# The last pair of heads moves into TensorE's loop, and two weight matrices are loaded ahead of its values

## Chip, cores and metric

One core of a Trainium2 chip. The time is that of one execution on the device in microseconds, as the median of several; the kernel before takes 687.5 us (three runs, 687.22 to 687.5). Everything is computed in f32.

## The reference, cut to what matters

```python
def _A_ref(x, k_cache, v_cache, wq, wo):          # x: 1 x 1 x 512; caches: 1 x 32 x 8192 x 128
    q = (x @ wq).reshape(B, Sq, H, Dh).transpose(0, 2, 1, 3)
    scores = jnp.einsum("bhqd,bhkd->bhqk", q, k_cache) * (Dh ** -0.5)
    p = _softmax(scores, axis=-1)
    o = jnp.einsum("bhqk,bhkd->bhqd", p, v_cache)
    return o.transpose(0, 2, 1, 3).reshape(B, Sq, H * Dh) @ wo

def _B_ref(x, w_gate, w_up, w_down):              # 512 x 1376, 512 x 1376, 1376 x 512
    h = _sigmoid(x @ w_gate) * (x @ w_up)
    return h @ w_down

xn = _layernorm(x)
return x + _A_ref(xn, ...) * _silu(_B_ref(xn, ...))
```

It decodes one token: attention of 32 heads over a cache of 8192 positions, times the silu of a gated unit. The two caches hold 268 MB of the 294 MB that are read.

## The kernel before

**Stages.** The heads are worked on in 16 pairs (NP = 16). A pair's keys and a pair's values are 8.39 MB each, laid out as 128 partitions of 64 KB, and fill one of three slots in the on-chip memory. Keys of pair i go to `slots[i % 2]`, values always to `slots[2]`, but for the last pair's. For each pair VectorE (DVE) multiplies the keys by the query and reduces (`scores`, L281 and L282; `summed[i]` marks the end and so that the slot of these keys is free). TensorE (PE) and ScalarE (ACT) make the maximum and the powers. PE multiplies 32 blocks of values by the weights into the PSUM bank `po` (L255, two passes for f32: 64 matmuls in the trace) and signals `valued`; ACT copies `po` to `o1` (`parts`, L301), PE picks the two heads' sums out of it (L260), DVE divides (`heads_out`), and ACT issues two small transfers that put the result into four partitions each of `o_all` (`place`, L131 on ACT's queue). The function `pair` holds PE's part. It runs 15 times in a hardware loop on PE and once more written out behind the loop.

**Order of the loads.** All large loads are issued by SP, in program order, each behind the wait that says that its slot is free:

```python
wait(SP, summed[NP - 2])
SP.dma_start(slots[NP % 2], rows_of(v_cache, NP - 1)).then_inc(v_last, 16)
...
ld_g = load(SP, "wg", wg_t, w_gate..., (valued, NP - 1))
```

So the last values go to `slots[0]`, free since the scores of pair 14 are done, and follow the values of pair 14 in the stream. Behind them come gate's matrix (2752 KB), up's (2752 KB) and down's (2560 KB, and its last 128 rows, 256 KB, again as `wd_last`) into `slots[2]`, which wait for the values of pair 14 to be used. Then the output matrix wo (8192 KB) in six pieces that end at rows 14, 24, 28, 30, 31 and 32 of each partition (`W_ENDS`), into `slots[1]`, which wait for the scores of pair 15. The program counts `valued` and `summed` so that `(valued, NP - 1)` is the end of pair 14's values.

**The end.** Behind the last pair PE multiplies by gate and up (L356; 64 matmuls of 320 columns and 48 of 32), DVE and ACT make the hidden vector and transpose it (L360 to L367), PE multiplies it by down (L384), ACT copies the four partial rows, PE folds them (L377, 8 matmuls) and the gate factor is made. Then PE waits for `placed[15]`, that is for `o_all`, and multiplies by wo piece by piece (L402 for rows 0 to 27 with 512 columns, four partial rows; a copy by ACT and a fold; L406 for rows 28 to 31 with 128 columns), each as it lands. DVE multiplies by the gate factor and adds x (L416, L418), and SP stores 2 KB.

Of the kernel before, what the change touches and what calls it, by code (L numbers as in the profile page):

```python
# [9 lines left out]
AF = mybir.ActivationFunctionType  # L10
# [3 lines left out]
P = 128  # L14
# [4 lines left out]
def kernel(  # L19
# [12 lines left out]
    nc = tc.nc  # L32
    _, H, S, Dh = k_cache.shape
    D = x.shape[-1]
    F = w_gate.shape[1]
    KT = D // P
    HP = P // 2
    NB = S // HP
    NP = H // 2
    NG = 4  # L40
    GP = P // NG
    GC = D // NG
    QT = 512
    HT = QT // Dh
    NQ = H * Dh // QT
# [6 lines left out]
    FP = F // P  # L52
    FL = F - FP * P
    FW = FP * GP
    FH = FW + GP
    assert FH <= QT and FL % GP == 0 and 2 * KT * F + FP * D <= SLOT

    W_ENDS, W_FOLD = (14, 24, 28, 30, 31, 32), 28

    PE, DVE, ACT, SP, POOL = nc.tensor, nc.vector, nc.scalar, nc.sync, nc.gpsimd  # L60
# [15 lines left out]
    x_col, xc, sq, xn = (sb(n, KT) for n in ("x_col", "xc", "sq", "xn"))  # L76
# [4 lines left out]
    slots = [sb(f"slot{i}", SLOT) for i in range(3)]  # L81
    x_row, g_row = sb("x_row", GC), sb("g_row", GC)
# [6 lines left out]
    wd_last = q_all[:, :D]  # L89
    sg, hg, s_tmp = (q_all[:, a:a + n] for a, n in ((D, FH), (D + FH, FH), (D + 2 * FH, QT)))  # L90
    assert D + 2 * FH + QT <= NP * Dh and FH <= QT

    weights = sb("weights", NB // HT, 2 * HT)
# [3 lines left out]
    hid = o1[:, :(FP + 1) * GP].rearrange("p (c i) -> p c i", i=GP)  # L97

    o_all = sb("o_all", WR)

    big = [bank(f"big{i}", P, QT) for i in range(2)]
    acc, po = bank("acc", P, GC), bank("po", P, QT)
# [6 lines left out]
    def semaphore(name):  # L109
        sems.append(nc.alloc_semaphore(name))  # L110
        return sems[-1]
# [11 lines left out]
    pe, dve, act, pool = (Steps(n) for n in ("s_pe", "s_dve", "s_act", "s_pool"))  # L123
    loads = {}

    def load(eng, name, dst, src, *after):
        wait(eng, *after)
        if name not in loads:
            loads[name] = [semaphore(f"s_{name}"), 0]
        loads[name][1] += 16  # L130
        eng.dma_start(dst, src).then_inc(loads[name][0], 16)  # L131
        return loads[name][0], loads[name][1]

    def wait(eng, *steps):
        for s in steps:
            if s is not None:
                eng.wait_ge(*s)


    turned, spread_m, valued, picked = (semaphore(f"s_{n}") for n in ("turned", "spread", "valued", "picked"))  # L140
    maxed, reduced, powers, copied = (semaphore(f"s_{n}") for n in ("maxed", "reduced", "powers", "copied"))
    s_val = semaphore("s_val")
# [6 lines left out]
    def rows_of(src, i):  # L149
        rows = src.rearrange("b h s d -> (b h s) d")[2 * i * S:2 * (i + 1) * S, :]  # L150
        return rows.rearrange("(p j) d -> p (j d)", p=P)
# [6 lines left out]
    def load_values(i, *after):  # L158

        wait(SP, *after)  # L160
        SP.dma_start(slots[2], rows_of(v_cache, i)).then_inc(s_val, 16)
# [10 lines left out]
    c_id = pool(POOL.memset(ident, 0.0))  # L172
    wait(POOL, c_id)
    c_id = pool(POOL.affine_select(out=ident, in_=ident, compare_op=ALU.not_equal, fill=1.0, base=0,
                                   pattern=[[-1, P]], channel_multiplier=1))
# [4 lines left out]
    t = dve(DVE.reduce_sum(st[:, 0:1], x_col, axis=AX.X))  # L180
    wait(PE, t)
    t = pe(PE.matmul(pt[:, 0:1], ones, st[:, 0:1], start=True, stop=True))  # L182
# [3 lines left out]
    t = dve(DVE.tensor_scalar(xc, x_col, st[:, 1:2], None, op0=ALU.subtract))  # L186
# [53 lines left out]
    def taken(sem, n):  # L240
        PE.wait_ge(sem, n)
        PE.nop().then_inc(sem, -n)  # L242

    def pair(v, loaded):
        taken(maxed, 1)
        PE.matmul(pt[0:1, :], mx[:, 0:1], ident, start=True, stop=True).then_inc(turned, 1)  # L246
        taken(reduced, 1)
        PE.matmul(pm, ones[:1, :], mx[:1, 1:3], start=True, stop=True).then_inc(spread_m, 1)  # L248
        taken(powers, 2)
        PE.matmul(pn[:, Dh:], half, rs, start=True, stop=True)  # L250
        loaded()

        for j in range(0, NB, HT):
            g = j // HT % NG
            ins = PE.matmul(po[g * GP:g * GP + 2 * HT, :], weights[:, j // HT, :], v[:, j * Dh:(j + HT) * Dh],  # L255
                            start=(j < HT * NG), stop=(j >= NB - HT * NG))
        ins.then_inc(valued, 1)
        taken(copied, 1)
        for b in range(HT):
            ins = PE.matmul(pn[:, :Dh], pick[:, b:2 * HT:HT], o1[:, b * Dh:(b + 1) * Dh],  # L260
                            start=(b == 0), stop=(b == HT - 1))
        ins.then_inc(picked, 1)

    wait(PE, c_pick, c_id)
    with nc.Fori(0, NP - 1, engines=OrderedEngineSet([PE.engine]), head_slot={PE.engine: 0}):
        pair(slots[2], lambda: taken(s_val, 16))

    v_last = semaphore("s_v_last")
    pair(slots[NP % 2], lambda: PE.wait_ge(v_last, 16))


    summed, outs, placed = {}, {}, {}
# [54 lines left out]
    place(NP - 1)  # L327


    wait(SP, summed[NP - 2])  # L330
    SP.dma_start(slots[NP % 2], rows_of(v_cache, NP - 1)).then_inc(v_last, 16)
    t = slots[2]
    wg_t, wu_t = (t[:, n * KT * F:(n + 1) * KT * F].rearrange("p (k f) -> p k f", f=F) for n in range(2))
    wd_t = t[:, 2 * KT * F:2 * KT * F + FP * D].rearrange("p (c e) -> p c e", e=D)
    ld_g = load(SP, "wg", wg_t, w_gate.rearrange("(p k) f -> p k f", k=KT), (valued, NP - 1))
    ld_u = load(SP, "wu", wu_t, w_up.rearrange("(p k) f -> p k f", k=KT))
    load(SP, "wd", wd_t, w_down[:FP * P, :].rearrange("(p r) e -> p r e", r=FP))
    ld_d = load(SP, "wd", wd_last, w_down[F - P:, :])
    wo_t = slots[(NP - 1) % 2].rearrange("p (r e) -> p r e", e=D)
    ld_o = []  # L340
    for n, (r0, r1) in enumerate(zip((0,) + W_ENDS, W_ENDS)):
# [1 line left out]
                         summed[NP - 1] if n == 0 else None))  # L343


    g0 = (P - FL) // GP
    wait(DVE, copies[NQ - 1])
    c_zero = dve(DVE.memset(big[1][:g0 * GP, FW:FH], 0.0))
    wait(PE, c_zero)
    rows = []  # L350
    for dst, src, ld in ((big[0], wg_t, ld_g), (big[1], wu_t, ld_u)):
        wait(PE, ld)
        for c0, f0, w, g1 in ((0, 0, FW, 0), (FW, F - P, GP, g0)):
            for k in range(KT):
                for g in range(g1, NG):
                    ins = PE.matmul(dst[g * GP:g * GP + 1, c0:c0 + w], xn[:, k:k + 1],  # L356
                                    src[:, k, f0 + g * w:f0 + (g + 1) * w], start=(k == 0), stop=(k == KT - 1))
        rows.append(pe(ins))
    wait(ACT, rows[0])
    t = act(ACT.activation(sg, big[0][:, :FH], AF.Sigmoid))  # L360
    wait(DVE, t, rows[1])
    c_p4 = dve(DVE.memset(big[0], 0.0))
    t = dve(DVE.tensor_mul(hg, sg, big[1][:, :FH]))
    wait(DVE, t)
    for c in range(FP):
        dve(DVE.transpose(hid[:, c, :], hg[:, c:FW:FP]))
    t = dve(DVE.transpose(hid[:, FP, :], hg[:, FW:]))  # L367

    def to_fold(after):
        wait(ACT, after)  # L370
        return act(ACT.copy(s_tmp, big[0]))

    def fold(dst, copied, last):

        wait(PE, copied)
        for g in range(NG):
            ins = PE.matmul(dst[g * GP:g * GP + 1, :GC], ones[:, 0:1], s_tmp[:, g * GC:(g + 1) * GC],  # L377
                            start=last, stop=last)
        return ins

    wait(PE, t, ld_d)
    for c in range(FP + 1):
        g = c % NG * GP
        ins = PE.matmul(big[0][g:g + 1, :], hid[:, c, 0:1], wd_t[:, c, :] if c < FP else wd_last,  # L384
                        start=(c < NG), stop=(c + NG > FP))
    t = to_fold(pe(ins))
    wait(DVE, t)
    c_acc4 = dve(DVE.memset(big[0], 0.0))
    wait(ACT, pe(fold(big[1], t, True)))
    t = act(ACT.activation(g_row, big[1][:, :GC], AF.Sigmoid))  # L390
    wait(DVE, t)
    c_gate = dve(DVE.tensor_mul(g_row, g_row, big[1][:, :GC]))


    wait(PE, c_acc4, placed[NP - 2], placed[NP - 1])
    r0, parts = 0, None
    for ld, r1 in zip(ld_o, W_ENDS):
        wait(PE, ld)
        for r in range(r0, r1):
            if r < W_FOLD:  # L400
                g = r % NG * GP
                ins = PE.matmul(big[0][g:g + 1, :], o_all[:, r:r + 1], wo_t[:, r, :],  # L402
                                start=(r < NG), stop=(r + NG >= W_FOLD))
                continue
            for g in range(NG):
                ins = PE.matmul(acc[g * GP:g * GP + 1, :], o_all[:, r:r + 1], wo_t[:, r, g * GC:(g + 1) * GC],  # L406
                                start=(r == W_FOLD), stop=(r == WR - 1))
        if parts is not None:

            fold(acc, parts, False)  # L410
            parts = None
        if r1 == W_FOLD:
            parts = to_fold(pe(ins))
        r0 = r1
    wait(DVE, pe(ins), c_gate, ld_xr)
    t = dve(DVE.tensor_mul(g_row, g_row, acc))  # L416
    wait(DVE, t)
# [40 lines left out]
```

## Time and profile before

| what | value |
|---|---|
| median of 3 runs | 687.5 us |
| the profiled execution's own time | 687.36 us |
| its span, first to last instruction | 685.6 us |
| around the span | 1.76 us |
| busy: PE, DVE, ACT | 32%, 84%, 6% of the span |
| DMA, mean over the span | 429 GB/s |
| granted clock of PE, mean over the span | 0.664 of full speed |

Times below are microseconds from the span's start. PE is TensorE's matmuls, PEld its loads of weights, SPq and ACTq the queues on which SP and ACT issue transfers; q1 is SP's queue on the 16 DMA engines and q10 ACT's. In a timeline, rows give start, length, engine, line, operation, target and sources, count, and in brackets the engine's idle time before and what ended it; a row with a count spans several instructions, and its length is their busy time.

### The profile page before, as it was taken

The numbers are of one execution on the slowest core, as the hardware profiler recorded it, in microseconds if no ns is written. First come the engines' busy times: TensorE is split into PE (matmuls) and PEld (weight loads), VectorE is DVE, ScalarE is ACT, GpSimd is POOL, SyncE is SP. The second block draws the span as 40 slices with busy tenths as digits, with TensorE's granted clock in tenths as the row PEclk, the third lists the DMA queues.
The fourth block names the chain that finished last, engine by engine and source line by source line (L and its number), as shares of the span: only waits on it lengthen the run. The fifth ranks groups of instructions, "written<-read, shape, count | busy, mean of one in ns | idle before, by whom it ended". The sixth has DMA issues, their size and how long they took to land.

```text
span 685.6 us, 3694 instructions
## 1 busy us (share of the span) xinstructions
PE 222.1 (32%) x1570; PEld 62.7 (9%) x1570; DVE 574.0 (84%) x136; ACT 40.9 (6%) x122; POOL 0.7 (0%) x6
## 2 busy tenths in 40 slices
PE   0550230605041140505042140506042140605656
PEld 0110000101010010101001010101000010101121
DVE  0159999999999999989898989989898989989220
ACT  0040100000000000000001010000001010000010
POOL 0000000000000000000000000000000000000000
PEclk9965575757566575757557575756657575756798
DMA  9999999999999999999999999999999999999996
GB/s 375 440 445 451 428 428 428 432 428 428 428 436 444 448 440 428 428 428 436 428 428 428 440 444 451 428 432 428 432 432 428 428 440 436 451 436 428 405 434 285
DMA packets 6614, 293.84 MB, mean 429 GB/s; under 512 B 1096, under 2 KB 1104, under 8 KB 1616
## 3 DMA queue, kind: packets, MB, share of 16 engines
q1 hardware_dynamic: 6200, 293.74, 99.1%
q10 hardware_dynamic: 408, 0.02, 0.0%
q8 instruction: 4, 0.07, 0.0%
q14 instruction: 2, 0.02, 0.0%
HBM read 293.74 MB, written 0.00 MB: 428 GB/s over the span
## 4 chain that ended last, share of the span: by engine, by line
DMA 37%; DVE 30%; PE 0%; SPq 0%; issue 0%
DMA slot<-in_A_k_cache_dram 31%; DVE slot L281 15%; DVE sc L282 15%; DMA slot<-in_A_wo_dram 6%; PE acc L406 0%; SPq L131 0%; PE pt L246 0%; PE acc L377 0%; DVE g_row L416 0%; DVE g_row L418 0%; DVE mx L276 0%
## 5 line engine op out<-in xcount | busy, mean ns | idle before, releaser
L281 DVE TENSOR_TENSOR slot<-slot,q_all 128x16384 f32<-128x16384 f32 x16 | 275.5, 17217 | 38.8 <-DMA slot<-in_A_k_cache_dram 38.8
L282 DVE TENSOR_REDUCE sc<-slot 128x128 f32<-128x16384 f32 x16 | 275.5, 17220 | 0.6
L255 PE MATMUL po<-slot,weights 128*8 128x512 f32 x1024 | 146.7, 737 | 232.1 <-PEq L242 231.5
L255 PEld LDWEIGHTS po<-slot,weights 128*8 128x8 f32 x1024 | 30.3, 103 | 335.3 <-issue 334.6
L246 PE MATMUL pt<-ident,mx 128*1 128x128 f32 x32 | 8.8, 374 | 148.6 <-PEq L242 148.6
L301 ACT COPY o<-po 128x512 f32<-128x512 f32 x16 | 9.4, 586 | 385.2 <-PE po L255 385.2
L260 PE MATMUL pn<-o,pick 128*2 128x128 f32 x128 | 16.5, 272 | 12.8 <-PEq L242 12.8
L180 DVE TENSOR_REDUCE st<-x_col 128x1 f32<-128x4 f32 x1 | 0.2, 157 | 20.7 <-DMA x_col<-in_A_x_dram 20.7
L246 PEld LDWEIGHTS pt<-ident,mx 128*1 128x1 f32 x32 | 1.8, 80 | 154.1 <-issue 154.1
L288 DVE RECIPROCAL rl<-pn 2x1 f32<-2x1 f32 x16 | 2.3, 146 | 14.6 <-PE pn L260 14.6
L294 ACT ACTIVATE nb<-pm 128x2 f32<-128x2 f32 x16 | 2.8, 173 | 190.4 <-PE pm L248 190.4
L416 DVE TENSOR_TENSOR g_row<-g_row,acc 128x128 f32<-128x128 f32 x1 | 0.3, 289 | 15.3 <-PE acc L406 15.3
L296 ACT ACTIVATE weights<-sc,nb 64x128 f32<-64x128 f32 x32 | 12.8, 399 | 0.9
L260 PEld LDWEIGHTS pn<-o,pick 128*2 128x2 f32 x128 | 9.9, 84 | 29.6 <-issue 27.2
L248 PE MATMUL pm<-mx,ones 1*128 1x2 f32 x32 | 8.8, 344 | 7.4 <-PEq L242 7.4
L402 PE MATMUL big<-slot,o_all 128*1 128x512 f32 x56 | 9.4, 765 | 4.8 <-DMA slot<-in_A_wo_dram 4.8
L250 PE MATMUL pn<-rs,half 128*2 128x1 f32 x32 | 3.0, 163 | 23.5 <-PEq L242 23.5
L218 PE MATMUL big<-q_all,ones 1*128 1x512 f32 x16 | 8.8, 850 | 1.6 <-ACT q_all L225 0.8
L206 PE MATMUL big<-slot,xn 128*1 128x512 f32 x64 | 9.0, 726 | 0.8 <-DVE xn L198 0.8
L248 PEld LDWEIGHTS pm<-mx,ones 1*128 1x128 f32 x32 | 7.9, 306 | 14.4 <-issue 14.4
L276 DVE TENSOR_REDUCE mx<-pt 1x2 f32<-1x128 f32 x16 | 4.5, 278 | 5.2 <-PE pt L246 5.0
L182 PE MATMUL pt<-st,ones 128*128 128x1 f32 x2 | 0.6, 362 | 23.4 <-DVE st L180 23.4
(61 smaller groups left out, 62.1 us busy)
## 6 DMA issues: line engine op xcount, KB each, us to landing
slot<-in_A_wo_dram SPq DMA_DIRECT2D x1, 3584.0 KB, 32.5
slot<-in_B_w_gate_dram SPq DMA_DIRECT2D x1, 2752.0 KB, 16.8
slot<-in_B_w_up_dram SPq DMA_DIRECT2D x1, 2752.0 KB, 22.8
slot<-in_B_w_down_dram SPq DMA_DIRECT2D x1, 2560.0 KB, 27.3
slot<-in_A_wo_dram SPq DMA_DIRECT2D x1, 2560.0 KB, 38.2
slot<-in_A_wo_dram SPq DMA_DIRECT2D x1, 1024.0 KB, 40.2
o_all<-on ACTq DMA_DIRECT2D x32, 0.5 KB
slot<-in_A_wo_dram SPq DMA_DIRECT2D x1, 512.0 KB, 40.9
```

Of the source, the lines that this page charges most:

```text
L206: ins = PE.matmul(big[b][g * GP:g * GP + 1, :], xn[:, k:k + 1], wq_t[:, k, c:c + QT], start=(k == 0), stop=(k == KT - 1))
L218: spreads[t] = pe(PE.matmul(big[t % 2], ones[g * GP:g * GP + 1, :], q_row[g * GP:g * GP + 1, b, :], start=True, stop=True))
L246: PE.matmul(pt[0:1, :], mx[:, 0:1], ident, start=True, stop=True).then_inc(turned, 1)
L248: PE.matmul(pm, ones[:1, :], mx[:1, 1:3], start=True, stop=True).then_inc(spread_m, 1)
L255: ins = PE.matmul(po[g * GP:g * GP + 2 * HT, :], weights[:, j // HT, :], v[:, j * Dh:(j + HT) * Dh], start=(j < HT * NG), stop=(j >= NB - ...
L260: ins = PE.matmul(pn[:, :Dh], pick[:, b:2 * HT:HT], o1[:, b * Dh:(b + 1) * Dh], start=(b == 0), stop=(b == HT - 1))
L276: DVE.reduce_max(mx[:1, 1:3], pt[0:1, :].rearrange("o (e p) -> o e p", e=2), axis=AX.X).then_inc(reduced, 1)
L281: wait(DVE, dve(DVE.tensor_mul(k, k, qb[:, i:i + 1, :].to_broadcast([P, NB, Dh]))))
L282: summed[i] = dve(DVE.reduce_sum(sc[i % 2], k, axis=AX.X))
L296: ACT.activation(weights[h, :, e * HT:(e + 1) * HT], sc[i % 2][h].rearrange("p (g b) -> p g b", b=HT), AF.Exp, bias=nb[h, e:e + 1], scale= ...
L301: ACT.copy(o1, po).then_inc(copied, 1)
L402: ins = PE.matmul(big[0][g:g + 1, :], o_all[:, r:r + 1], wo_t[:, r, :], start=(r < NG), stop=(r + NG >= W_FOLD))
```

## The change

The last pair is the sixteenth turn of PE's loop (head slot 64 in its block of code instead of 0). Its values go to `slots[2]` like all others, so they wait for pair 14's values to be used. Gate's and up's matrices, and `wd_last`, go ahead of them in SP's order, into `slots[0]`, and wait for pair 14's scores; the rest of down's follows the last values, then wo as before. Gate and up take 64 matmuls in all, the last row group with 416 columns instead of separate narrow matmuls; the last 96 entries of the hidden vector need three transposes of 32 x 32. wo's first 28 rows gather in `po` instead of `big[0]`; on PE its piece of rows 0 to 13 comes ahead of down's matmuls, and the piece of rows 14 to 23 between down's and the fold.

```diff
-    FH = FW + GP
+    FH = FW + FL
...
-    def pair(v, loaded):
+    wait(PE, c_pick, c_id)
+    with nc.Fori(0, NP, engines=OrderedEngineSet([PE.engine]), head_slot={PE.engine: 64}):
         taken(maxed, 1)
         PE.matmul(pt[0:1, :], mx[:, 0:1], ident, start=True, stop=True).then_inc(turned, 1)
         taken(reduced, 1)
         PE.matmul(pm, ones[:1, :], mx[:1, 1:3], start=True, stop=True).then_inc(spread_m, 1)
         taken(powers, 2)
         PE.matmul(pn[:, Dh:], half, rs, start=True, stop=True)
-        loaded()
+        taken(s_val, 16)
 
         for j in range(0, NB, HT):
             g = j // HT % NG
-            ins = PE.matmul(po[g * GP:g * GP + 2 * HT, :], weights[:, j // HT, :], v[:, j * Dh:(j + HT) * Dh],
+            ins = PE.matmul(po[g * GP:g * GP + 2 * HT, :], weights[:, j // HT, :],
+                            slots[2][:, j * Dh:(j + HT) * Dh],
...
-
-    wait(PE, c_pick, c_id)
-    with nc.Fori(0, NP - 1, engines=OrderedEngineSet([PE.engine]), head_slot={PE.engine: 0}):
-        pair(slots[2], lambda: taken(s_val, 16))
-
-    v_last = semaphore("s_v_last")
-    pair(slots[NP % 2], lambda: PE.wait_ge(v_last, 16))
...
-    wait(SP, summed[NP - 2])
-    SP.dma_start(slots[NP % 2], rows_of(v_cache, NP - 1)).then_inc(v_last, 16)
-    t = slots[2]
+    t = slots[NP % 2]
     wg_t, wu_t = (t[:, n * KT * F:(n + 1) * KT * F].rearrange("p (k f) -> p k f", f=F) for n in range(2))
     wd_t = t[:, 2 * KT * F:2 * KT * F + FP * D].rearrange("p (c e) -> p c e", e=D)
-    ld_g = load(SP, "wg", wg_t, w_gate.rearrange("(p k) f -> p k f", k=KT), (valued, NP - 1))
+    ld_g = load(SP, "wg", wg_t, w_gate.rearrange("(p k) f -> p k f", k=KT), summed[NP - 2])
     ld_u = load(SP, "wu", wu_t, w_up.rearrange("(p k) f -> p k f", k=KT))
-    load(SP, "wd", wd_t, w_down[:FP * P, :].rearrange("(p r) e -> p r e", r=FP))
-    ld_d = load(SP, "wd", wd_last, w_down[F - P:, :])
+    ld_l = load(SP, "wd_last", wd_last, w_down[F - P:, :])
+    load_values(NP - 1, (valued, NP - 1))
+    ld_d = load(SP, "wd", wd_t, w_down[:FP * P, :].rearrange("(p r) e -> p r e", r=FP))
...
-    g0 = (P - FL) // GP
-    wait(DVE, copies[NQ - 1])
-    c_zero = dve(DVE.memset(big[1][:g0 * GP, FW:FH], 0.0))
-    wait(PE, c_zero)
+    wait(PE, copies[NQ - 1])
     rows = []
     for dst, src, ld in ((big[0], wg_t, ld_g), (big[1], wu_t, ld_u)):
         wait(PE, ld)
-        for c0, f0, w, g1 in ((0, 0, FW, 0), (FW, F - P, GP, g0)):
-            for k in range(KT):
-                for g in range(g1, NG):
-                    ins = PE.matmul(dst[g * GP:g * GP + 1, c0:c0 + w], xn[:, k:k + 1],
-                                    src[:, k, f0 + g * w:f0 + (g + 1) * w], start=(k == 0), stop=(k == KT - 1))
+        for k in range(KT):
+            for g in range(NG):
+                w = FH if g == NG - 1 else FW
+                ins = PE.matmul(dst[g * GP:g * GP + 1, :w], xn[:, k:k + 1], src[:, k, g * FW:g * FW + w],
+                                start=(k == 0), stop=(k == KT - 1))
         rows.append(pe(ins))
+
+    dve(DVE.memset(hid[:, FP, :], 0.0))
+    c_po = dve(DVE.memset(po, 0.0))
...
-    wait(DVE, t)
+    wait(DVE, t, c_po)
     for c in range(FP):
         dve(DVE.transpose(hid[:, c, :], hg[:, c:FW:FP]))
-    t = dve(DVE.transpose(hid[:, FP, :], hg[:, FW:]))
-
-    def to_fold(after):
+    for n in range(FL // GP):
+
+        p0 = P - FL + n * GP
+        c_hid = dve(DVE.transpose(hid[p0:p0 + GP, FP, :], hg[P - GP:, FW + n * GP:FW + (n + 1) * GP]))
+
+    def to_fold(src, after):
         wait(ACT, after)
-        return act(ACT.copy(s_tmp, big[0]))
+        return act(ACT.copy(s_tmp, src))
...
-    wait(PE, t, ld_d)
-    for c in range(FP + 1):
-        g = c % NG * GP
-        ins = PE.matmul(big[0][g:g + 1, :], hid[:, c, 0:1], wd_t[:, c, :] if c < FP else wd_last,
-                        start=(c < NG), stop=(c + NG > FP))
-    t = to_fold(pe(ins))
-    wait(DVE, t)
-    c_acc4 = dve(DVE.memset(big[0], 0.0))
-    wait(ACT, pe(fold(big[1], t, True)))
-    t = act(ACT.activation(g_row, big[1][:, :GC], AF.Sigmoid))
-    wait(DVE, t)
-    c_gate = dve(DVE.tensor_mul(g_row, g_row, big[1][:, :GC]))
-
-
-    wait(PE, c_acc4, placed[NP - 2], placed[NP - 1])
-    r0, parts = 0, None
-    for ld, r1 in zip(ld_o, W_ENDS):
-        wait(PE, ld)
+    def project(r0, r1):
         for r in range(r0, r1):
             if r < W_FOLD:
                 g = r % NG * GP
-                ins = PE.matmul(big[0][g:g + 1, :], o_all[:, r:r + 1], wo_t[:, r, :],
+                ins = PE.matmul(po[g:g + 1, :], o_all[:, r:r + 1], wo_t[:, r, :],
...
+
+    wait(PE, c_po, placed[NP - 2], placed[NP - 1], ld_o[0])
+    project(0, W_ENDS[0])
+    wait(PE, c_hid, c_p4, ld_l, ld_d)
+    for c in range(FP + 1):
+        g = c % NG * GP
+        ins = PE.matmul(big[0][g:g + 1, :], hid[:, c, 0:1], wd_t[:, c, :] if c < FP else wd_last,
+                        start=(c < NG), stop=(c + NG > FP))
+    t = to_fold(big[0], pe(ins))
+    wait(PE, ld_o[1])
+    project(W_ENDS[0], W_ENDS[1])
+    wait(ACT, pe(fold(big[1], t, True)))
+    t = act(ACT.activation(g_row, big[1][:, :GC], AF.Sigmoid))
+    wait(DVE, t)
+    c_gate = dve(DVE.tensor_mul(g_row, g_row, big[1][:, :GC]))
+    parts = None
+    for ld, r0, r1 in zip(ld_o[2:], W_ENDS[1:], W_ENDS[2:]):
+        wait(PE, ld)
+        ins = project(r0, r1)
         if parts is not None:
 
             fold(acc, parts, False)
             parts = None
         if r1 == W_FOLD:
-            parts = to_fold(pe(ins))
-        r0 = r1
+            parts = to_fold(po, pe(ins))
```

## Rows read from the trace of the kernel before

**Rows 1.** Chain that ended last, in order of time: start, length, what.

```profile
639.57 40.94 DMA slot<-in_A_wo_dram
...
681.82 0.44 PE acc L406 x8
...
682.28 0.30 DVE g_row L416
```

**Rows 2.** Timeline of SP's queue: start, length, line, target, count.

```profile
599.59 0.33 SPq L331 DMA_DIRECT2D slot<-in_A_v_cache_dram  x1
632.49 0.33 SPq L131 DMA_DIRECT2D slot<-in_B_w_gate_dram  x1
632.86 0.43 SPq L131 DMA_DIRECT2D slot<-in_B_w_up_dram  x1
...
633.81 0.43 SPq L131 DMA_DIRECT2D q_all<-in_B_w_down_dram  x1
638.25 11.93 SPq L131 DMA_DIRECT2D slot<-in_A_wo_dram  x6
```

**Rows 3.** DMA issues: size and time from issue to landing.

```profile
slot<-in_B_w_gate_dram SPq DMA_DIRECT2D x1, 2752.0 KB, 16.8
slot<-in_B_w_up_dram SPq DMA_DIRECT2D x1, 2752.0 KB, 22.8
...
q_all<-in_B_w_down_dram SPq DMA_DIRECT2D x1, 256.0 KB, 28.5
...
x_col<-in_A_x_dram ACTq DMA_DIRECT2D x1, 2.0 KB, 22.1
```

**Rows 4.** Timeline of PE alone, 60 to 640 us: matmuls with values, pick.

```profile
82.09 8.42 PE L255 MATMUL po<-slot,weights 128*8 128x512 f32 x64 [0.40 <-PEq L242]
...
623.21 9.21 PE L255 MATMUL po<-slot,weights 128*8 128x512 f32 x64 [20.21 <-PEq L242]
633.22 1.03 PE L260 MATMUL pn<-o,pick 128*2 128x128 f32 x8 [0.80 <-PEq L242]
```

**Rows 5.** Timeline of all engines, 632 to 666 us.

```profile
632.49 0.59 ACT L301 COPY o<-po 128x512 f32<-128x512 f32 x1 [29.83 <-PE po L255]
...
642.44 9.84 PE L255 MATMUL po<-slot,weights 128*8 128x512 f32 x64 [0.57 <-DMA slot<-in_A_v_cache_dram]
...
654.71 1.19 ACTq L131 DMA_DIRECT2D o_all<-on  x2
...
654.83 4.96 PE L356 MATMUL big<-slot,xn 128*1 128x320 f32 x112 [0.71 <-DVE big L348]
...
660.05 0.48 DVE L362 MEMSET big<- 128x512 f32 x1 [5.28 <-PE big L356]
...
662.46 2.31 PE L384 MATMUL big<-slot,o 128*1 128x512 f32 x18 [2.68 <-DVE o L367]
...
665.26 0.59 ACT L371 COPY q_all<-big 128x512 f32<-128x512 f32 x1 [7.35 <-PE big L384]
```

**Rows 6.** Timeline of all engines, 670 to 682 us.

```profile
670.91 5.81 PE L402 MATMUL big<-slot,o_all 128*1 128x512 f32 x28 [4.61 <-DMA slot<-in_A_wo_dram]
...
676.87 3.60 PE L402 MATMUL big<-slot,o_all 128*1 128x512 f32 x28 [0.15 <-DMA slot<-in_A_wo_dram]
677.30 0.10 PEld L402 LDWEIGHTS big<-slot,o_all 128*1 128x1 f32 x4 [0.33 <-issue]
...
681.16 0.40 PE L377 MATMUL acc<-q_all,ones 128*1 128x128 f32 x8
```

**Rows 7.** DMA queues, 654.7 to 661.25 us: ACT's queue.

```profile
q10 hardware_dynamic: 16, 0.00, 0.2%
```

**Rows 8.** DMA queues, 661 to 661.25 us: ACT's queue.

```profile
q10 hardware_dynamic: 1, 0.00, 0.2%
```

**Rows 9.** Windows of half a microsecond; granted clock is third from the end.

```profile
668.00:668.50 0.50, 0.00 (x0) 0.00 (x0) 0.00 (x0) 0.00 (x0) 0.00 (x0) 1.00 0.93 401
668.50:669.00 0.50, 0.00 (x0) 0.00 (x0) 0.00 (x0) 0.00 (x0) 0.00 (x0) 0.57 0.75 320
```

More of the change, by code (lines that the diff above doesn't have):

```diff
@@ L407 @@
                                 start=(r == W_FOLD), stop=(r == WR - 1))
+        return ins
+    wait(PE, c_po, placed[NP - 2], placed[NP - 1], ld_o[0])
[16 more added lines that the diff above has]
+        ins = project(r0, r1)
         if parts is not None:
```

## The prediction

> **What bounds the kernel now.** First the busy shares and the DMA rate of the table ahead: 429 GB/s as a mean over the whole span, with DVE at 84% and PE at 32%. Then the chain of waits: it ends on the transfers: 40.94 us of it are the stream that brings wo; behind its last piece come 0.44 us of PE and then DVE's product at 682.28 [rows 1]. So at the end PE waits for each piece of wo as it lands, as the brackets of its rows say [rows 6], and everything earlier on PE is hidden. A change of order can't shorten a stream that never pauses. It can only put a pause into it, or put PE behind it. So I read the tail twice: when does each transfer land, and how much work is left for PE behind the last big one?
>
> Now the values of pair 14 have landed when PE starts at 623.21 [rows 4], those of pair 15 at about 642.4 (PE starts at 642.44, released by the transfer) [rows 5]. From their issues at 632.49, 632.86 and 633.81 gate lands at 649.3, up at 655.7, `wd_last` at 662.3 [rows 2, 3]. So 28.5 us of transfers come behind the last values until wo's first piece at 670.9 [rows 6], and PE does pair 15, gate, up and down (654.83 to 665.26) [rows 5] under them, and then idles until 670.91 [rows 6]. This slack is what the change spends.
>
> **The stream in the new order.** The same bytes. Gate, up and `wd_last` can be issued at 599.59, where the last values are issued now (same wait, `summed[14]`) [rows 2], and follow pair 14's values. Gate and up take 655.7 - 642.4 = 13.3 us, `wd_last` by its bytes 0.6 (256 of the 2816 KB that take 662.3 - 655.7 = 6.6 us) [rows 3, 5]. They end at 623.2 + 13.9 = 637.1. Pair 15's values wait for `valued` of pair 14, as gate does now: 632.49 [rows 2]. That is 4.6 us before the queue is empty, so I cost this wait at nothing. Its cover is pair 14's duration on PE: 9.21 us here, 8.42 at the least [rows 4]; at the low clock throughout it would be 64 matmuls at the 5.81 us for 28 of wo's first piece [rows 6], 13.3 us, and the wait would end at 636.5, 0.6 ahead of the end: a pause would be at most the time that a transfer needs to start. On the same engine queue, down and wo are behind this wait; both are due long after it.
>
> Pair 15's values land 13.9 us later than now: 656.3. Down and wo follow as before, and wo's last piece lands at the same time as now, just before 681.8. The stream gives nothing and loses nothing. What is new: from 656.3 PE has pair 15, gate, up, down and all of wo to do in the 25.5 us until the stream ends.
>
> **PE's chain behind 656.3.** Full-clock rate: four matmuls of 512 columns in 0.43 us (0.10 + 0.33); at the low clock 0.83 (5.81 for 28) [rows 6].
> - Pair 15: 9.2 us, the value of pair 14, between 8.42 and 9.84 [rows 4, 5]: 665.5. Inside the loop it is the same code.
> - Copy and pick: from pair 14's last matmul at 632.4 to 633.22 + 1.03 = 634.25, 1.8 us [rows 4, 5]: 667.3.
> - Gate and up: now 4.96 us for 64 wide and 48 narrow matmuls [rows 5]; then 64, a quarter of them with 416 columns. Below: the same 4.96. Above: 4.96 x 416 / 320 = 6.4, if the widest sets the pace. I take 5.5: 672.9.
> - `place` of pair 15: now ACT issues it at 654.71, 2.4 us behind the last value matmul at 652.3 [rows 5]; then at 667.9. When does it land? ACT's queue moved 16 packets between 654.7 and 661.25, and the last of them within the last quarter of a microsecond [rows 7, 8]: 6.4 us from the first issue. I take 6.6, since it meets wo's packets of 28 and 20 KB, and then met 22 and 20 KB and some of 2 KB: 674.5. The far bound above is a small transfer on this queue behind packets of 64 KB, 22.1 us [rows 3]; below, the first issue's own length, about 0.6. Now this wait is hidden under 16 us (654.71 to 670.91); in the new order it is late, and PE stands from 672.9 to 674.5.
>
> The Trainium skill (DMA: Bandwidth & Descriptors, Anatomy of one DMA) gives a fixed cost of about 2.0 us per transfer, fitted on GpSimd's path. By it `place` would be there before gate and up are done and the stall would be nothing; by the 6.4 us of the rows there is one. The page's section on queues and rings says that each DMA engine takes whole packets from its queues in turn, which would explain such a delay. I go by the rows, and keep the short landing as a rival.
>
> - wo rows 0 to 13, 28 matmuls, 7 groups of 0.43: 3.0 us, to 677.5. Now it takes 5.81 us, since the clock is low after PE's idle time of 4.61 us from 666.3 (granted 1.00 until 668.5, 0.57 in the next half microsecond) [rows 6, 9]. In the new order PE has worked since 656.3 but for the stall of 1.6 us, so I take the full clock.
> - Down: 22 matmuls, 2.4 us, to 679.9; its input is ready, since gate and up end at 672.9 and DVE's part took 662.46 - 660.05 = 2.4 us and takes about 0.4 more (wider product, two more transposes) [rows 5]. ACT's copy of 0.59 is hidden under the next piece.
> - wo rows 14 to 23, 20 matmuls, 2.15 us: 682.05. The first fold, 8 small matmuls, 0.2 when nothing waits for its end (0.40 with its last result) [rows 6]: 682.25.
> - wo rows 24 to 27, 8 matmuls: 0.75 to the start of the last and some 0.6 for its result (the difference of start and copy in the row of down, 2.8 us for 22 matmuls of 2.4, is of that kind) [rows 5]: 683.6. ACT's copy with its waits 0.7: 684.3.
> - Second fold 0.40, the eight matmuls of row 30 0.2, those of row 31 0.44 [rows 1, 6]: 685.35. DVE starts at 685.4.
>
> Now that is 682.28 [rows 1], so +3.1 us. The execution profiled took 687.36 (span 685.6 and 1.76 around it): 687.36 + 3.1 = 690.5. It stands 0.14 below the median shown, which I leave out.
>
> The other edits lie beside this chain. The memsets of `po` and `hid` run on DVE while PE does gate; the narrow matmuls that go are in the 4.96 us. The end of the loop now lies directly ahead of gate: no wait for code is seen in the rows, so nothing; its upper bound is again the 6.4 us of a small transfer in a full stream.
>
> **Rivals.** Within 0.2% (1.4 us) a measurement of this kernel can't tell a change.
> 1. Forecast: PE late by its chain with the stall on `place`. 690.5, own range 689.2 to 692. Chance 0.60.
> 2. `place` lands within 5 us of its issue: no stall. The chain is 1.6 us shorter, 688.9; with gate and up at 5.0, 688.4. Against it: 6.4 us in the rows. 0.15, half of it within 0.2%.
> 3. The stall lets the clock fall. wo's first piece takes 5.81 instead of 3.0: 693.3. For it: the clock had fallen 2.7 us after PE's last work in [rows 9]; against it: the stall that I expect is 1.6 us. 0.12.
> 4. Not slower: PE keeps up. This takes `place` landed by 671.4 (3.1 us sooner) and gate done by then too, with pair 15 at 8.42. The end is then the stream's: 687.4; if the stream behind 642.4, 16.9 MB in 39.4 us or 429 GB/s, ran at the 437 of pair 15's values (8.39 MB in 19.2 us), 0.7 sooner, 686.7. 0.07, mostly within 0.2%; faster needs more than that.
> 5. The queue runs empty ahead of pair 15's values (pair 14 at the low clock throughout), or PE waits for code behind the loop: 1 to 6 us more, 691.5 to 697. 0.06.
>
> **The numbers.** The likeliest is 690.5. The range from 687.9 to 693.4 takes in the forecast, most of 2 and 3, and part of 5; out stay most of 4 and the upper part of 5. Slower: 0.60 + 0.12 + 0.06 and half of 2, less some of the forecast's lower edge: 0.81. Within 0.2%: 0.15. Faster: 0.04.
>
> **What would show it.** Right: PE's L255 of pair 15 starts at about 656; PE's wait ahead of the first wo matmuls ends with ACT's queue and not with wo's piece, at about 674.5; no wait for wo's pieces behind it; DVE's last product at about 685.4; SP's issue of the last values near 632.8 and no hole in the DMA row between 635 and 640. Wrong: PE waiting for wo's last pieces again, as in [rows 6]; a hole in the stream; or PE's matmuls at 0.83 per four behind 668.

## The result, and the profile after

The kernel after takes 690.94 us (median of 6, 690.31 to 691.9) beside 687.43 of the kernel before (6 runs): ratio 1.005, 95% interval 1.004 to 1.0061. Slower by 3.5 us, as forecast (690.5, range 687.9 to 693.4). The profiled execution took 691.9, the longest of the six; that matters below.

The page of after: the bytes read, and the chain that ended last by engine.

```profile
HBM read 293.74 MB, written 0.00 MB: 426 GB/s over the span
...
PE 3%; DVE 0%; ACT 0%; issue 0%; DVEq 0%
```

The bytes are the same (293.74 MB before too). The chain no longer ends on wo's stream: DMA isn't in its line of engines at all, where before the chain went back through 40.94 us of that stream [rows 1]. The page shows only the last stretch of it, 3% on PE, and misses a wait for a transfer in it, as the timeline below shows.

SP's queue of after, start and length:

```profile
599.46 0.33 SPq L131 DMA_DIRECT2D slot<-in_B_w_gate_dram  x1
...
632.63 0.33 SPq L161 DMA_DIRECT2D slot<-in_A_v_cache_dram  x1
...
638.12 2.70 SPq L131 DMA_DIRECT2D slot<-in_A_wo_dram  x6
```

Gate goes out at 599.46, where the last values went before; these go at 632.63, as gate did [rows 2]. wo's burst goes at 638.12 against 638.25, and its pieces land where they did: the page gives 32.9 us from issue to landing for the first (32.5 before) and 38.4 for the second (38.2). The stream's last packet ends at 681.4 before and 681.5 in after: the stream has neither gained nor lost.

Timeline of all engines of after, and behind it ACT's queue of transfers from 673.5 to 674.0 us:

```profile
656.08 8.37 PE L256 MATMUL po<-slot,weights 128*8 128x512 f32 x64 [14.33 <-PEq L242]
...
666.12 5.55 PE L347 MATMUL big<-slot,xn 128*1 128x320 f32 x61
...
666.88 1.19 ACTq L131 DMA_DIRECT2D o_all<-on  x2
...
674.23 0.68 DVE L364 STREAM_TRANSPOSE o<-q_all 32x32 f32<-32x32 f32 x3
...
674.54 4.87 PE L382 MATMUL po<-slot,o_all 128*1 128x512 f32 x26 [2.87 <-DVE o L364]
...
686.83 0.29 DVE L416 TENSOR_TENSOR g_row<-g_row,acc 128x128 f32<-128x128 f32 x1 [1.81 <-PE acc L386]
```

```profile
q10 hardware_dynamic: 3, 0.00, 0.3%
```

The last values start on PE at 656.08, 13.6 us later than before [rows 5]. Gate and up end at 671.7. PE then stands 2.87 us until 674.54. The profile puts this wait down to DVE's transposes, and the rows rule that out: the last of the three ends at 674.91 (674.23 + 0.68), behind PE's start. What the code waits for there is a memset of `po`, which ended at 667.5, wo's first piece, which landed at 671.0 (638.12 + 32.9), and the two small transfers; ACT's queue moved the last three packets of these from 673.5 on, the last at 673.97. Run 3 takes the transfers out of this wait, run 4 takes the transposes away. None of wo's pieces is waited for behind it, and DVE's product comes at 686.83 against 682.28 [rows 1]: +4.55 in this execution.

Windows of 1 us of after; the granted clock is third from the end:

```profile
674.00:675.00 1.00, 0.46 (x8) 0.17 (x12) 0.81 (x5) 0.00 (x0) 0.00 (x0) 1.00 0.91 389
675.00:676.00 1.00, 1.00 (x16) 0.30 (x12) 0.00 (x0) 0.00 (x0) 0.00 (x0) 0.93 0.90 381
676.00:677.00 1.00, 1.00 (x11) 0.17 (x4) 0.00 (x0) 0.00 (x0) 0.00 (x0) 0.50 0.99 418
...
680.00:681.00 1.00, 1.00 (x16) 0.25 (x11) 0.00 (x0) 0.00 (x0) 0.00 (x0) 1.00 0.40 152
```

The clock fell behind the stall, when PE had begun again: 1.00 from 674 to 675, 0.93 as the mean of the next microsecond, 0.50 (the lower of the two levels, 1.2 GHz) from 676 on, 1.00 again at 680.

### The profile page after: what moved, and what is told of

Its sections match the earlier page's. It is cut to its first block, busy times and chain, and to the rows that moved or that the text cites. A ratio compares the mean times of both kernels' runs of the same rounds, so it can differ in the third digit from the quotient of the medians.

```text
span 690.1 us, 3605 instructions
## 1 busy us (share of the span) xinstructions
PE 219.3 (32%) x1522; PEld 63.2 (9%) x1522; DVE 574.6 (83%) x138; ACT 40.9 (6%) x122; POOL 0.7 (0%) x6
## 3 DMA queue, kind: packets, MB, share of 16 engines
q1 hardware_dynamic: 6200, 293.74, 98.4%
HBM read 293.74 MB, written 0.00 MB: 426 GB/s over the span
## 5 line engine op out<-in xcount | busy, mean ns | idle before, releaser
L382 PE MATMUL po<-slot,o_all 128*1 128x512 f32 x56 | 10.0, 708 | 2.9 <-DVE o L364 2.9
## 6 DMA issues: line engine op xcount, KB each, us to landing
slot<-in_A_wo_dram SPq DMA_DIRECT2D x1, 3584.0 KB, 32.9
slot<-in_A_wo_dram SPq DMA_DIRECT2D x1, 2560.0 KB, 38.4
```

What stands on the lines that cost most here:

```text
L382: ins = PE.matmul(po[g:g + 1, :], o_all[:, r:r + 1], wo_t[:, r, :], start=(r < NG), stop=(r + NG >= W_FOLD))
```

## The experiments

All times are medians beside the kernel before on the same chip (687.4 to 687.5).

**1. The loads of before, the work order of after.** Loop, last pair and the order of SP's loads are put back; gate's 64 matmuls and wo's first rows ahead of down stay.

```diff
+    wait(SP, summed[NP - 2])
+    SP.dma_start(slots[NP % 2], rows_of(v_cache, NP - 1)).then_inc(v_last, 16)
...
-    ld_g = load(SP, "wg", wg_t, w_gate.rearrange("(p k) f -> p k f", k=KT), summed[NP - 2])
+    ld_g = load(SP, "wg", wg_t, w_gate.rearrange("(p k) f -> p k f", k=KT), (valued, NP - 1))
...
-    load_values(NP - 1, (valued, NP - 1))
```

> The new work order behind the last pair (gate in 64 matmuls, wo's first rows ahead of down's) with the loads and the loop of before. Theory (the loads' order makes PE late): the last values land at 642.4 again, PE waits for wo's pieces as before, time 687.4 within 0.5. Rival (the new work order itself costs): 689 to 691.

689.27 us, ratio 1.0024 (1.0014 to 1.0033): in the rival's range, and not the theory's 687.4, though the last values come early and PE waits for wo's first piece again, as the theory has it. Timeline of all engines:

```profile
642.66 8.38 PE L255 MATMUL po<-slot,weights 128*8 128x512 f32 x64 [0.50 <-DMA slot<-in_A_v_cache_dram]
...
671.03 5.67 PE L388 MATMUL po<-slot,o_all 128*1 128x512 f32 x26 [12.30 <-DMA slot<-in_A_wo_dram]
...
684.12 0.29 DVE L422 TENSOR_TENSOR g_row<-g_row,acc 128x128 f32<-128x128 f32 x1 [1.80 <-PE acc L392]
```

PE idles 12.30 us with gate and up done, for wo's first piece; down's matmuls, whose data have long been there, stand behind it in the program. From 671.03 PE needs 13.1 us to DVE's product at 684.12. Before it needed 11.4 (670.91 to 682.28) [rows 1, 6], since down and its fold were done. So the new work order has a price of its own, about 1.8 us, when the last values come early. Behind the long idle time wo's first matmuls run slowly (26 in 5.67 us, against 3.17 in run 4), so this is the price at that pace; no run shows it without the idle time.

**2. The loads and loop of after, the work order of before.** Gate's and up's narrow matmuls are back too.

```diff
-    wait(PE, c_po, placed[NP - 2], placed[NP - 1], ld_o[0])
-    project(0, W_ENDS[0])
-    wait(PE, c_hid, c_p4, ld_l, ld_d)
+    wait(PE, t, ld_l, ld_d)
...
+    wait(PE, c_acc4, placed[NP - 2], placed[NP - 1])
```

> The loads and the loop of after with the work order of before behind the last pair. Theory: the last values still land near 656; gate ends near 671.2, down's matmuls come behind DVE's part at about 674.2, then fold and 28 rows of wo in a row behind it: slower than before by 3 to 7 us, 690.5 to 694. Rival (the new work order itself costs): 687.4.

692.96 us, ratio 1.008 (1.0066 to 1.0094). As the theory expects.

```profile
656.45 8.77 PE L256 MATMUL po<-slot,weights 128*8 128x512 f32 x64 [14.58 <-PEq L242]
...
675.36 2.31 PE L378 MATMUL big<-slot,o 128*1 128x512 f32 x18 [2.63 <-DVE o L361]
...
678.16 0.59 ACT L365 COPY q_all<-big 128x512 f32<-128x512 f32 x1 [7.30 <-PE big L378]
...
679.47 6.19 PE L396 MATMUL big<-slot,o_all 128*1 128x512 f32 x56 [0.27 <-DVE big L382]
...
687.27 0.29 DVE L410 TENSOR_TENSOR g_row<-g_row,acc 128x128 f32<-128x128 f32 x1 [7.40 <-PE acc L400]
```

Here all 28 rows of wo (56 matmuls, 6.19 us) lie behind down and its fold. The loads alone cost 5.5 us; the new work order gives 2.0 of them back by the medians (692.96 against 690.94). The profiles show 1.3 us of it: from 675.36 run 2 takes 11.91 us to DVE's product, and run 5 below, from wo's first matmul at 675.32, takes 10.59. In run 2 PE does no matmuls of wo from ACT's copy at 678.16 until the fold and a memset are done at 679.47; in the new order such matmuls lie there. The rest of the 2.0 was not traced. So the sum of +3.5 is not a sum of two costs: each part alone is slower than before, and the second is a remedy for the first.

**3. wo's first rows without the small transfers.** They are multiplied by a constant column in place of `o_all`, which leaves out their part of the output.

```diff
-    wait(PE, c_po, placed[NP - 2], placed[NP - 1], ld_o[0])
-    project(0, W_ENDS[0])
+    wait(PE, c_po, ld_o[0])
+    project(0, W_ENDS[0], ones[:, 0:1])
```

> Leaves out wo's rows 0 to 13 as they should be: their matmuls take a constant column in place of o_all, so that the wait for the last pair's small transfers comes only behind down's matmuls. Theory (PE stands for the small transfers): the first wo matmuls start right behind gate, at about 671.7 instead of 674.5, the clock stays at its upper level, and the end comes 3 to 4.5 us sooner: 686.9 to 688.5. Rival (PE stands for DVE's last transpose, as the profile names it): start at 674.5 and 690.9, unchanged.

689.02 us, ratio 1.0022 (1.0013 to 1.0031): 1.9 us faster than after, less than the 3 to 4.5 expected.

```profile
671.19 0.81 PE L382 MATMUL po<-slot,ones 128*1 128x512 f32 x3
...
675.95 2.31 PE L396 MATMUL big<-slot,o 128*1 128x512 f32 x18 [0.72 <-DVE o L364]
...
683.94 0.29 DVE L416 TENSOR_TENSOR g_row<-g_row,acc 128x128 f32<-128x128 f32 x1 [1.80 <-PE acc L386]
```

wo starts with gate's last matmuls, at 671.19, and no stall is left there; what is late next is DVE's hidden vector: down waits 0.72 us for it, until 675.95. I had costed that as ready in time, which it is only while wo's first rows start late.

**4. Without the transposes.** Down is multiplied by what lies in `hid`; DVE is done 1.8 us earlier (673.10 against 674.91).

```diff
-    for c in range(FP):
-        dve(DVE.transpose(hid[:, c, :], hg[:, c:FW:FP]))
...
+    c_hid = t
```

> Leaves out the 13 transposes of the hidden vector, so down is multiplied by other numbers; DVE is done at about 672.9 instead of 674.4. Theory (PE stands for the small transfers): the first wo matmuls start at 674.5 as in after and the time is 690.9 within 0.7. Rival (PE stands for DVE's last transpose): start at 673.0, and 689.0 to 689.5.

690.77 us, ratio 1.0056 (1.004 to 1.0072): as after.

```profile
667.10 1.19 ACTq L131 DMA_DIRECT2D o_all<-on  x2
...
672.53 0.57 DVE L357 TENSOR_TENSOR q_all<-q_all,big 128x416 f32<-128x416 f32 x1
...
674.47 3.17 PE L377 MATMUL po<-slot,o_all 128*1 128x512 f32 x26 [2.58 <-DMA o_all<-on]
...
685.06 0.29 DVE L411 TENSOR_TENSOR g_row<-g_row,acc 128x128 f32<-128x128 f32 x1 [1.70 <-PE acc L381]
```

DVE ends at 673.1 and wo's first matmul still starts at 674.47; now the profile names the transfer, DMA o_all<-on. With run 3 this shows that PE stands for the small transfers, 7.4 us behind their issue at 667.10. The clock did not fall here: from 674.47 to DVE's product at 685.06 it takes 10.59 us.

**5. PE kept busy in the stall**, by 32 matmuls on constants into an unused bank.

```diff
+    for n in range(32):
+        g = n % NG * GP
+        PE.matmul(pt[g:g + 1, :], ones[:, 0:1], ident, start=True, stop=True)
```

> 32 more matmuls of 128 columns on constants, into an unused bank, behind gate and up, so that PE works through most of its stall; the result is not touched. Theory (the stall lets the clock fall, as it did from 675.9 to 679.1 in the trace of after): granted clock 1.00 throughout 666 to 686, the end up to 1.6 us sooner in executions where it fell, median 689.3 to 690.4. Rival (the clock costs nothing at the end, or the extra matmuls delay PE): 690.9 or later.

691.12 us, ratio 1.005 (1.0037 to 1.0064): no gain in the median, as the rival has it.

```profile
667.78 1.19 ACTq L131 DMA_DIRECT2D o_all<-on  x2
...
675.32 3.17 PE L382 MATMUL po<-slot,o_all 128*1 128x512 f32 x26 [1.01 <-DVE o L364]
...
685.91 0.29 DVE L419 TENSOR_TENSOR g_row<-g_row,acc 128x128 f32<-128x128 f32 x1 [1.80 <-PE acc L386]
```

From wo's first matmul to DVE's product it takes 10.59 us again, against 12.29 in the profile of after, so the fall of the clock cost that execution 1.7 us. But the median doesn't move. So the fall in the profile of after, its longest execution, is not what makes the median; how many executions have it was not measured.

**6. One small transfer instead of two.** The second head's part of `o_all` stays zero.

```diff
+    dve(DVE.memset(o_all, 0.0))
...
-    place(NP - 1)
+    p0 = 2 * (NP - 1) * WP
+    placed[NP - 1] = load(ACT, "place1", o_all[p0:p0 + WP, :],
+                          on[1][:1, :].rearrange("o (a r) -> o a r", r=WR), outs[NP - 1])
```

> Leaves out the small transfer of the last pair's second head (its part of the vector stays at the zeros set at the start). Theory (small packets take turns with the stream's in the same rings, so two transfers take twice the turns): from the issue to PE's first wo matmul 5 to 6 us instead of 7.4 to 7.6, and since DVE's part ends only some 0.1 to 0.2 us ahead of that start, down's matmuls still begin behind wo's first rows: 688.5 to 689.8. Rival (the landing is a fixed delay per transfer): 6.8 us or more, by the second issue of 0.6 that is gone, 690.2 to 690.9.

689.58 us, ratio 1.0029 (1.0019 to 1.0039): 1.4 us faster than after.

```profile
668.36 0.58 ACTq L131 DMA_DIRECT2D o_all<-on  x1
...
674.06 3.17 PE L385 MATMUL po<-slot,o_all 128*1 128x512 f32 x26 [0.92 <-DVE big L359]
...
684.65 0.29 DVE L419 TENSOR_TENSOR g_row<-g_row,acc 128x128 f32<-128x128 f32 x1 [1.80 <-PE acc L389]
```

From issue to PE's start 5.70 us instead of 7.4 to 7.7; the profile names DVE again, with a memset that wo's rows don't wait for. The second transfer costs more than its 0.6 us of issue.

The reason is in the packets that the traces hold. Each of these transfers is eight packets on ACT's queue: four of 128 bytes and, behind each, one of 4 bytes. The two transfers together make four chains of four packets. Counts of packets in three stretches, each with all 16 of ACT's: after from 670.6 to 674.0 us, before from 605.7 to 615.0 (the transfers of pair 14) and before from 658.7 to 661.25 (those of pair 15):

```profile
DMA packets 86, 1.43 MB, mean 422 GB/s; under 512 B 16, under 2 KB 16, under 8 KB 16
...
DMA packets 79, 4.13 MB, mean 444 GB/s; under 512 B 16, under 2 KB 16, under 8 KB 16
...
DMA packets 193, 1.16 MB, mean 453 GB/s; under 512 B 44, under 2 KB 44, under 8 KB 154
```

In the first stretch all the stream's packets are of 20 KB, which take 0.76 us each, and the packets of a chain start 0.77 us apart (670.69, 671.46, 672.23, 672.99). In the second all are of 64 KB, 2.42 us each, and the steps are 2.42 us (605.81, 608.23, 610.65, 613.08). So one packet of the stream goes between two of ACT's, and a second transfer adds two steps to each chain: 1.53 us beside 20 KB packets. PE starts 0.56 to 0.58 us behind the last of ACT's packets in after (673.97) and in runs 4, 5, 6, 9 and 10, whichever engine the profile names.

**7. The last values ahead of gate and up, still in the third slot.**

```diff
+    load_values(NP - 1, (valued, NP - 1))
     ld_g = load(SP, "wg", wg_t, w_gate.rearrange("(p k) f -> p k f", k=KT), summed[NP - 2])
...
-    load_values(NP - 1, (valued, NP - 1))
```

> The last values go ahead of gate and up again, but into the third slot as in after, so they wait for the values of pair 14 to be used. Theory (gate and up in front only fill the time of that wait): the stream stands empty from 623 until about 634, PE starts the last values at about 653.5, the stream ends some 11 us later than before: 698 within 1.5. Rival (the wait is hidden anyway): 687.4 to 691.

702.02 us, ratio 1.0216 (1.02 to 1.0232): later than either range. The DMA row of 40 slices from 620 to 660 us, then the timeline:

```profile
DMA  3000000000009901909099090970909019988999
```

```profile
653.97 8.62 PE L256 MATMUL po<-slot,weights 128*8 128x512 f32 x64 [11.88 <-PEq L242]
...
683.45 5.35 PE L382 MATMUL po<-slot,o_all 128*1 128x512 f32 x26 [13.65 <-DMA slot<-in_A_wo_dram]
...
696.23 0.29 DVE L416 TENSOR_TENSOR g_row<-g_row,acc 128x128 f32<-128x128 f32 x1 [1.80 <-PE acc L386]
```

Nothing moves from 621 to 632: this is the hole that gate and up fill in after. wo's first piece is 12.5 us later than before (683.45 against 670.91 [rows 6]), which is 1.5 more than I had for the hole; the rest of the 14.6 agrees with the price of the work order that run 1 found (1.8), which I hadn't counted.

**8. Gate and up ahead of the last pair on PE**, which is written out again; wo's rows come behind down and the fold.

```diff
         rows.append(pe(ins))
+    pair(slots[2], lambda: taken(s_val, 16))
```

> The loads of after; on PE gate's and up's matmuls come ahead of the last pair's, which is written out behind the loop again, and wo's rows come behind down's and the fold. Theory (PE's chain behind the last values is what is late): gate and up are off the chain (5.8 us less), down starts near 669.5, wo waits for the small transfers until about 674: 1 to 3 us faster than after, 688 to 690. Rival (the small transfers don't hold PE): wo starts at 672.5, and 687.4 to 688.

692.85 us, ratio 1.0077 (1.0063 to 1.009). Both theories missed it, and the edit is why:

```profile
638.83 0.86 PE L349 MATMUL big<-slot,xn 128*1 128x416 f32 x2
...
669.07 1.19 ACTq L131 DMA_DIRECT2D o_all<-on  x2
...
671.59 0.52 ACT L357 ACTIVATE q_all<-big 128x416 f32<-128x416 f32 x1
...
674.58 0.68 DVE L367 STREAM_TRANSPOSE o<-q_all 32x32 f32<-32x32 f32 x3
...
675.32 4.14 PE L397 MATMUL big<-slot,o 128*1 128x512 f32 x18 [6.85 <-DVE o L367]
...
680.83 6.19 PE L385 MATMUL po<-slot,o_all 128*1 128x512 f32 x56
...
688.63 0.29 DVE L419 TENSOR_TENSOR g_row<-g_row,acc 128x128 f32<-128x128 f32 x1 [6.97 <-PE acc L389]
```

PE was done with gate and up by 640, but ACT's sigmoid stood behind the issue of the small transfers and a table load (669.07 to 672.1), so DVE's transposes ended at 675.3, down began at 675.32, at the lower clock (18 matmuls in 4.14 us, against 2.31 in run 2), and wo behind it.

**9 and 10. The sigmoid and the transposes ahead too** (run 9), and 40 matmuls on constants before wo's wait (run 10). `hid` moves from `o1`'s place to that of `s_tmp`, so that it can be written before the last pair is done.

```diff
-    hid = o1[:, :(FP + 1) * GP].rearrange("p (c i) -> p c i", i=GP)
+    hid = s_tmp[:, :(FP + 1) * GP].rearrange("p (c i) -> p c i", i=GP)
...
+    parts(NP - 1)
+    heads_out(NP - 1)
+    place(NP - 1)
     def to_fold(src, after):
```

> The loads of after; gate, up, the sigmoid and the transposes all come ahead of the last values, so that behind them PE has only pair 15, down and wo. Theory (what is left late is the small transfer, 7.4 us behind its issue): wo's first matmuls wait until 674.5 to 676 with PE idle and its clock falling, DVE's last product near 684 to 686.5, time 689 to 692: not better than before although 8 us of work have left the chain. Rival (PE's work behind the last values is all of it): 687.4.

> The kernel of the run before with 40 matmuls of 128 columns on constants ahead of the wait for the small transfers; the result is not touched. Theory (clock): granted clock higher when wo's first rows run, 0.5 to 2.5 us sooner than without them: 687.5 to 690. Rival (the clock has no part): no change against the run before.

Run 9 takes 690.57 us, ratio 1.0046 (1.0032 to 1.006); run 10 688.27, ratio 1.0015 (1.0006 to 1.0024). Timelines of run 9 and run 10:

```profile
667.42 1.20 ACTq L131 DMA_DIRECT2D o_all<-on  x2
...
674.51 9.07 PE L386 MATMUL po<-slot,o_all 128*1 128x512 f32 x56 [4.01 <-DMA o_all<-on]
...
685.20 0.29 DVE L420 TENSOR_TENSOR g_row<-g_row,acc 128x128 f32<-128x128 f32 x1 [14.03 <-PE acc L390]
```

```profile
670.92 2.37 PE L407 MATMUL pt<-ident,ones 128*1 128x128 f32 x80
...
675.36 6.19 PE L386 MATMUL po<-slot,o_all 128*1 128x512 f32 x56 [2.08 <-DMA o_all<-on]
...
683.16 0.29 DVE L423 TENSOR_TENSOR g_row<-g_row,acc 128x128 f32<-128x128 f32 x1 [11.39 <-PE acc L390]
```

With gate, up, hidden vector and down's wait off the chain, PE is done with down and its fold at 670.5 and stands 4.01 us for the small transfers, 7.1 us behind their issue; its clock falls (granted 0.50 from 673.5 to 680.4), and 56 matmuls take 9.07 us. Kept busy it does them in 6.19. Both times are in the theories' ranges. Here the clock is worth 2.3 us in the median (690.57 to 688.27), unlike in run 5. No version came out faster than the kernel before, which waits for the stream's last byte. That the new order of loads can at best come back to that is argued from the unchanged stream, not shown.

## Why the prediction was right

- **The stream.** Forecast: unchanged, the wait for `valued` hidden, last values at 656.3. Measured: 656.08 to 656.45 in after and runs 2 to 6, wo as before. Right; run 7 shows the hole that would be there without gate and up.
- **Pair 15.** 9.2 us forecast, 8.37 in the profile of after, 8.49 to 9.56 in runs 2 to 6. Inside the bounds taken.
- **Gate and up.** 5.5 forecast, 5.76 measured (665.91 to 671.67); the first of them overlap the last pick. The widest matmuls didn't set the pace alone (6.4).
- **The small transfers.** Start of wo forecast at 674.5, measured at 674.54, but by two errors that cancel, which is luck: the issue came 1.0 earlier (666.88 against 667.9), the way to PE's start took 7.7 us instead of 6.6, and the stall 2.87 instead of 1.6. The mechanism holds: runs 3, 4 and 6 show that this wait is real, at 5.70 us for one transfer and 7.1 to 7.7 for two. So rival 2 falls. The Trainium skill (DMA: Bandwidth & Descriptors, Anatomy of one DMA) gives a fixed cost of about 2.0 us for one transfer, fitted on GpSimd's path; the traces here, on ACT's queue beside the stream, don't agree with it (5.70 us at the least).
- **Why 7.7 and not 6.6.** The forecast took the 6.4 us to the last packet from [rows 7, 8] and 0.2 for all behind it; measured in after are 7.1 and 0.57. Before, three of the four chains ended with a step of under 0.1 us, where the stream moved mostly the 2 KB packets of `wd_last` (0.08 us each); so the chain that began last, at 659.38, was done at 660.25, where full steps would have taken it to 661.68, 7.0 us behind the issue. In after `wd_last` is long through, and every step is 0.77 us. That the small packets are the reason fits these rows and was not tested alone. wo's packets of 28 KB, which the prediction reckoned with, are over before the first chain begins.
- **Down's input.** Forecast as ready, with 2.8 us for DVE's part behind gate; it took 3.24 (671.67 to 674.91). In after this is hidden, since wo's rows start late; in run 3 it costs 0.72 us.
- **From there to the end.** 10.9 forecast (674.5 to 685.4), 10.59 measured in runs 4 and 5 with the clock up. Rival 3, the falling clock, came true in the profiled execution in part (1.7 of its 2.8 us) and not in the median.
- **Rival 4** was priced too low. Run 3 gives it most of what it asks for, wo's rows that start right behind gate, and takes 689.02; with pair 15 at the 8.42 that it names instead of run 3's 9.10 that would be 688.3 by estimate, not 687.4. Run 1 (689.27) doesn't test it, since wo's matmuls are slow there behind 12.30 us of idle time. I had costed the work order as part of the chain and not asked what it does alone.
- **The code behind the loop.** Gate's first matmul starts at 665.91 while the picks still run, so no wait for code.

Open: what makes up the 3.7 to 4.9 us from the issue to the first packet of each chain in after and the runs, and why the clock fell in the profile of after and not in those of runs 4 to 6.

## What to carry to other kernels

When transfers bound a kernel, a change of their order is judged by the work that is left behind the last large landing: here 13.6 us later meant that PE's chain (pair, gate, small transfers, wo) outlasted the stream, of which some 25 us were left, where before there were some 39 to hide under. Each small transfer that was hidden under 16 us becomes a term of that chain at its price beside a full stream: here some 4 us to its first packets, and then one packet of the stream for each of its own. And when a wait is for several things, the engine that the profile names is a guess: look whether its last instruction ended before the wait did, and take one of the things away.

## What was not expected of the hardware

Two transfers of 0.5 KB beside the stream took 7.1 to 7.7 us from the first issue to PE's start, one took 5.70; their packets wait for one packet of the stream each, 0.77 us at 20 KB and 2.42 us at 64 KB. The clock fell in the profile of after behind a stall of 2.87 us (674.54 start, 0.50 from 676), and not in runs 4 and 5 with stalls of 2.58 and 1.01 us. SP's burst of six issues of wo took 2.70 us in after, 11.93 before [rows 2] and 22.94 in run 7; whether that costs anything was not tested.
